# Head bits from four column tiles, TensorE's order rewritten, and a different start of a 16-head attention with two MLPs

## Chip, core and metric

The kernel runs on one core of one Trainium2 chip. The metric is the device time of one execution in microseconds (us).

## What is computed

Attention whose mask comes from hashing: queries and keys are projected on six directions, the signs of the projections are six bits, and a query sees only the keys with the same six bits. Two MLPs follow. In the reference (cut):

```python
# batch 2, heads 8, sequence 768, head_dim 64; x is (1536, 512)
q_bits = (np.einsum('bhsd,dk->bhsk', q, proj) > 0)          # 6 bits, k the same
mask = q_bucket[:, :, :, None] == k_bucket[:, :, None, :]
scores = np.where(mask, (1/8) * np.matmul(q, k.T), -1e9)
attn = softmax(scores)
x = np.matmul(attn, v)                                       # heads side by side
h = np.maximum(np.maximum(x @ w1, x @ w2), x @ w3) @ w_out   # 512 -> 768 -> 512
g = h2 >= 1 ? h2 : h2 <= -1 ? 0 : (h2 + 1)**2 / 4            # h2 = h @ w_in, 512 -> 2048
return g @ w_out2                                            # 2048 -> 512
```

## The kernel before

**Stages.** The attention runs first (to about 189 us), the MLPs after it. A head (16 in all) has six tiles of 128 queries by 768 keys. Its inputs come as one array `r` with k in rows 0 to 63 and q in rows 64 to 127. Each number is split into a rounded part `hi` and a rest `lo`, so that products in the fast format keep their precision; `q`, `hi` and `lo` of a head are put together on 128 rows by transfers on SP's queue (`prep_both`: `q<-hi`, `prep_move`: `q<-lo`, `lo<-hi`).

**Bits.** `bits_both` multiplies `r` with the projection: two products of 384 columns each (a head's two halves), with 64 result rows each, in two column tiles of TensorE. `bits_rows` compares them on VectorE, once per half (44 rows by 384), and writes 44 rows of `q`; 12 of them are the query's bits and already in place, the key's 12 go to `hi` by one transfer on SP's queue (`hi<-q`, 12 rows by 768). The bits then stand as 12 more rows of the tile's product, where unequal bits add a huge number.

**A tile.** `t_qk` (L414, L417) makes four products of 384 columns in one of two PSUM buffers `s_ps`; `t_max` (VectorE, L424) takes the row's minimum and copies the tile out; `t_exp` (ScalarE, L439); then either six transposes (`t_tr`, L447, "t" below), copies out (`t_out`), and products with v (`g_pv`, L508, in two parts of 4 and 8 products with two passes each); or, for heads 2, 4, ... 14, a transpose on VectorE (`t_turn`) and one block of 96 small products (`block4`, L475: 32 rows by 64 columns of the array, 192 result columns each).

**Order.** A planner (`Work`) places tasks by costs and due times, but TensorE's own order is written out by hand in three strings (`first_part`, `period`, `last_part`): `q7` is the tile at place 7 of the sequence, `t7` its transposes, `v5` and `w5` the two parts of the products with v after tile 5, `b5` a head's bits, `B` head 1's bits, `r` a small transpose. The tile at place 6 is the first of head 1, that at place 10 the first of head 2, that at place 15 the first of head 3.

**Start.** TensorE first makes 13 products on zeros in bf16 (`warm_up`), while GpSimd changes signs in the projection `pj_raw` and scales it to `pj_sc`; head 0's two bit products follow, one after the other since both use the same column tile, then head 0's moves on ScalarE and GpSimd, with four more `warm_up` products between the first tile's own.

Of the kernel before, what the change touches and what calls it, by code (L numbers as in the profile page):

```python
# [8 lines left out]
F32 = mybir.dt.float32  # L9
# [4 lines left out]
ALU = mybir.AluOpType  # L14
# [8 lines left out]
HALF = S // 2  # L23
MASKED = 1.0e9
# [89 lines left out]
def lsh_attention_moe_kernel(  # L114
# [29 lines left out]
    pj_raw = const.tile([128, 64], F32, name="pj_raw")  # L144
# [3 lines left out]
    sc_sb = const.tile([128, 1], F32, name="sc_sb")  # L148
    one_exp = const.tile([128, 1], F32, name="one_exp")
# [131 lines left out]
    def attention(mlp_steps):  # L281
        with ExitStack() as ax, ExitStack() as sx:
# [24 lines left out]


# [18 lines left out]
            def pj_sign():  # L327
                for c0 in (0, 32):
                    nc.gpsimd.tensor_scalar(
                        out=pj_raw[:, c0:c0 + 6], in0=pj_raw[:, c0:c0 + 6], scalar1=-1.0, scalar2=0.0, op0=ALU.mult, op1=ALU.add  # L330
                    )
                nc.gpsimd.tensor_scalar(
                    out=pj_sc, in0=pj_raw, scalar1=sc_sb, scalar2=0.0, op0=ALU.mult, op1=ALU.add
                )
# [54 lines left out]
            def bits_mm(h, half, bank, first):  # L389
                nc.tensor.matmul(  # L390
                    out=bank[first:first + 64, 0:HALF], lhsT=pj_raw if h else pj_sc,
                    rhs=head[h]["r"][:, half * HALF:(half + 1) * HALF], start=True, stop=True,
                )
# [8 lines left out]
            def bits_both(h):  # L402
                for half in range(2):
                    bits_mm(h, half, pj_ps, 64 * half)


            def t_qk(n, bank):
# [3 lines left out]
                for half in range(2):  # L411
# [3 lines left out]
                    if n == 0:  # L415
                        warm_up(4, half)
# [73 lines left out]
            ahead = s_ps[1][:, 0]  # L490
# [107 lines left out]
            warm_up(13, 0)  # L598
            load_head(1)
            load_v(0)  # L600
            banks0 = (pj_ps, u_ps)
            halves = [slice(0, HALF), slice(HALF, S)]
            pj_sign()
            prep_hi_scaled(0, halves[0])
            bits_mm(0, 0, banks0[0], 64)
            prep_lo_scaled(0, 0, nc.vector)
            prep_move(0, "qb", nc.gpsimd.tensor_copy, halves[0])
            prep_hi_scaled(0, halves[1])
            bits_mm(0, 1, banks0[1], 64)
            prep_move(0, "qa", nc.scalar.copy, halves[0])  # L610
            prep_move(0, "ql", nc.scalar.copy, halves[0])
            prep_lo_scaled(0, 1, nc.vector)
            prep_move(0, "kh", nc.gpsimd.tensor_copy, halves[0])
            bits_rows(0, 0, banks0[0], 64)
            prep_move(0, "ql", nc.scalar.copy, halves[1])
            prep_move(0, "qb", nc.gpsimd.tensor_copy, halves[1])
            prep_move(0, "qa", nc.scalar.copy, halves[1])
            prep_move(0, "kh", nc.gpsimd.tensor_copy, halves[1])
            prep_move(0, "kb", nc.scalar.copy, halves[0])
            bits_rows(0, 1, banks0[1], 64)  # L620
            prep_move(0, "kb", nc.scalar.copy, halves[1])

            work = Work()
            T_AT, P_AT = 2, 1
            START = {h: min(SLOT[NK * h + t] for t in range(NK)) for h in range(NH)}
# [4 lines left out]
            SHIFT = {t_exp: 42.5, t_out: 2.0, g_copy: 17.5, copy4: -82.0, pair_copy: -20.5, w_tick: 60.0, bits_rows: 4.5, t_max: -12.5, t_turn: 8.0, pair_recip: 20.0}  # L630
# [8 lines left out]
            scaled, moves, r_place, order = {}, {}, {}, {}  # L639
            raw_s["prep"].free.pop()  # L640
            raw_s["r"].free.pop()

            def head_tasks(h):
# [17 lines left out]
                scaled[h], moves[h], r_place[h] = hi, [q, ql, kh], rp  # L661
                if h == 1:
                    bp = place("b", 1)
                    mm = task("PE", 0.644, due + 1, bits_both, h, after=[hi], takes=[bp], leaves=[rp])
                    order["bits"] = [mm]
                    rows = [
                        task("DVE", 0.69, due + 1, bits_rows, h, half, pj_ps, 64 * half, after=[mm]) for half in range(2)
                    ]
                    rows[1]["leaves"] = [bp]
                    bits_task(h, rows, due + 1)  # L670

            def bits_task(h, rows, due):
# [426 lines left out]
```

## Time and profile before

| | us |
|---|---|
| median of 3 runs (lowest, highest) | 667.93 (667.04, 668.33) |
| the profiled execution's own time | 668.48 |
| its span, first to last instruction | 666.6 |
| TensorE busy in the span | 657.4 |
| VectorE, ScalarE, GpSimd busy | 486.2, 341.0, 274.4 |

The difference of 1.9 us between the execution's time and its span lies around the program. PE is TensorE, DVE VectorE, ACT ScalarE, POOL GpSimd, SP the engine that issues most transfers. TensorE's products are pipelined: a row's time includes the last product's way through the array, so what a step takes is read from its start to the next row's start. A float32 product is two passes and shows as two records.

### The profile page before, as it was taken

How to read it: one execution, taken by the hardware profiler on the slowest of the kernel's cores; microseconds unless marked ns; L12 is line 12 of the kernel's file. 1: busy time of each engine (PE TensorE's matmuls, PEld its weight loads, DVE VectorE, ACT ScalarE, POOL GpSimd, SP SyncE). 2: the span in 40 equal slices, each digit the busy share in tenths (PEclk: the TensorE clock that was granted, in tenths of full speed). 3: DMA queues.
4: the chain of work that ended last, by engine and by line, in shares of the span. 5: the costliest groups of instructions: out<-in, count | busy, mean ns of one | idle time of the engine just before them, and what ended most of it. 6: DMA issues, size and time to landing. Idle time of an engine off the chain costs nothing.

```text
span 666.6 us, 11523 instructions
## 1 busy us (share of the span) xinstructions
PE 657.4 (99%) x4419; PEld 527.4 (79%) x4419; DVE 486.2 (73%) x717; ACT 341.0 (51%) x633; POOL 274.4 (41%) x249
## 2 busy tenths in 40 slices
PE   8999999999999999999999999999999999999998
PEld 5667777777867888888888888888888888888886
DVE  5787989998863667875453466766888888888844
ACT  7787877887782233333222325665444444444430
POOL 5436556766322335344223113644444444444430
PEclk9999999999999999999999999999999999999999
DMA  6847787775243122322111122121111222211004
GB/s 194 221 122 185 199 217 197 186 243 140 83 135 81 64 95 72 119 70 65 47 49 56 55 73 86 42 71 57 63 64 64 63 65 63 64 63 64 32 0 190
DMA packets 27855, 66.99 MB, mean 100 GB/s; under 512 B 4164, under 2 KB 9124, under 8 KB 27800
## 3 DMA queue, kind: packets, MB, share of 16 engines
q1 hardware_dynamic: 27488, 66.21, 33.8%
q8 instruction: 35, 0.57, 0.4%
q14 instruction: 20, 0.16, 0.1%
q10 hardware_dynamic: 312, 0.04, 0.0%
HBM read 46.17 MB, written 3.19 MB: 74 GB/s over the span
## 4 chain that ended last, share of the span: by engine, by line
PE 96%; issue 1%; DVE 1%; DMA 1%; ACT 1%; SPq 0%; POOL 0%; POOLq 0%; DVEq 0%
PE b L270 49%; PE b L1017 20%; PE s_ps L414 6%; PE t_ps L447 5%; PE u_ps L508 5%; PE s_ps L417 5%; PE u_ps L475 3%; PE pj_ps L390 2%; PE t_ps L475 1%; DVE p L424 1%; DMA rb<-d 0%; PE pj_ps L475 0%; ACT p L439 0%; PE s_ps L270 0%; DMA d<-rt 0%
## 5 line engine op out<-in xcount | busy, mean ns | idle before, releaser
L270 PE MATMUL b<-x_hl,wx 128*128 128x512 f32 x684 | 159.6, 389 | 0.0
L270 PEld LDWEIGHTS b<-x_hl,wx 128*128 128x128 f32 x684 | 128.4, 188 | 26.6
L270 PE MATMUL b<-x_hl,w 128*128 128x512 f32 (+1 forms) x564 | 123.8, 376 | 0.0
L270 PEld LDWEIGHTS b<-x_hl,w 128*128 128x128 f32 x564 | 100.9, 188 | 19.8 <-issue 0.6
L917 POOL TENSOR_TENSOR g<-r,g 128x512 fp32r<-128x512 f32 x48 | 62.5, 1304 | 121.4 <-ACT g L916 121.4
L424 DVE TENSOR_SCALAR_CACHE_REDUCE p<-s_ps 128x768 f32<-128x768 f32 x96 | 89.7, 951 | 11.9 <-PE s_ps L417 8.7
L206 DVE SCALAR_TENSOR_TENSOR wg<-wg,wr 128x512 f32<-128x512 f32 (+1 forms) x58 | 67.3, 1160 | 37.6 <-ACT wg L204 36.9
L439 ACT ACTIVATE p<-p,nm 128x768 f32<-128x768 f32 x96 | 89.7, 936 | 5.6 <-DVE p L424 5.1
L414 PE MATMUL s_ps<-lo,q 128*128 128x384 f32 x192 | 72.0, 375 | 1.0 <-DVE p L424 0.9
L233 POOL TENSOR_TENSOR wx<-wg,wx 128x512 fp32r<-128x512 f32 (+1 forms) x32 | 45.6, 1426 | 65.3 <-ACT wx L227 48.4
L1017 PE MATMUL b<-wx,g 128*128 128x512 f32 x288 | 72.1, 389 | 0.0
L1017 PE MATMUL b<-w,g 128*128 128x512 f32 (+1 forms) x294 | 71.3, 385 | 0.0
L227 ACT CAST wx<-wg 128x512 fp32r<-128x512 f32 (+1 forms) x32 | 19.3, 604 | 92.6 <-DVE wg L219 92.6
L417 PE MATMUL s_ps<-hi,q 76*128 76x384 f32 x192 | 65.3, 340 | 0.0
L997 DVE SCALAR_TENSOR_TENSOR r<-r,b 128x512 f32<-128x512 f32 x48 | 33.0, 687 | 44.3 <-ACT r L996 44.3
L1017 PEld LDWEIGHTS b<-w,g 128*128 128x128 f32 x294 | 54.5, 188 | 11.1
L1017 PEld LDWEIGHTS b<-wx,g 128*128 128x128 f32 x288 | 54.1, 188 | 11.2
L1024 DVE TENSOR_TENSOR acc<-b,acc 128x512 f32<-128x512 f32 (+1 forms) x85 | 56.3, 675 | 7.7 <-PE b L1017 7.6
L233 POOL TENSOR_TENSOR w<-wg,w 128x512 fp32r<-128x512 f32 (+1 forms) x26 | 35.9, 1382 | 49.3 <-ACT w L227 39.1
L211 DVE TENSOR_SCALAR wg<-wg 128x512 int32<-128x512 int32 (+1 forms) x58 | 53.3, 920 | 2.7
L995 ACT ACTIVATE r<-b,half_sb 128x512 f32<-128x512 f32 x48 | 33.0, 687 | 41.3 <-PE b L270 41.3
L227 ACT CAST w<-wg 128x512 fp32r<-128x512 f32 (+1 forms) x26 | 15.8, 608 | 74.0 <-DVE wg L219 74.0
(90 smaller groups left out, 1060.2 us busy)
## 6 DMA issues: line engine op xcount, KB each, us to landing
wr<-in_w SPq DMA_DIRECT2D x48, 512.0 KB
r<-in_kq SPq DMA_DIRECT2D x15, 384.0 KB
q<-hi SPq DMA_DIRECT2D x15, 384.0 KB
v<-in_v SPq DMA_DIRECT2D x21, 256.0 KB
rb<-d SPq DMA_DIRECT2D x16, 192.0 KB
wr<-in_w SPq DMA_DIRECT2D x8, 384.0 KB
q<-lo SPq DMA_DIRECT2D x15, 192.0 KB
lo<-hi SPq DMA_DIRECT2D x15, 192.0 KB
```

The source lines that it names most:

```text
L206: nc.vector.scalar_tensor_tensor(out=f32(g), in0=f32(g), scalar=TINY_SQ, in1=f32(high), op0=ALU.is_ge, op1=ALU.mult)
L211: nc.vector.tensor_scalar(out=g2, in0=g, scalar1=3, scalar2=0x3FFFFFF8, op0=ALU.logical_shift_left, op1=ALU.bitwise_and)
L227: nc.scalar.copy(out=w[:, 0, 0:cols], in_=f32(g2))
L233: nc.gpsimd.tensor_tensor(out=w[:, 1, 0:cols], in0=f32(g2), in1=f32(w[:, 0, 0:cols]), op=ALU.subtract)
L270: nc.tensor.matmul(out=outp, lhsT=w_[a], rhs=x_[b_], start=(begins and i == 0 and jj == 0), stop=(ends and i == n - 1 and jj == 2),)
L414: nc.tensor.matmul(out=o, lhsT=hd["qa"][:, qs], rhs=hd["lo"][:, ks], start=True, stop=False)
L417: nc.tensor.matmul(out=o, lhsT=hd["qb"][0:76, qs], rhs=hd["hi"][0:76, ks], start=False, stop=True)
L424: nc.vector.tensor_scalar(out=p.rearrange("p (a k) -> p a k", a=2), in0=s_ps[bank.at][:, :, 0:HALF], scalar1=MASKED, scalar2=MASKED, op0=A ...
L439: nc.scalar.activation(out=p, in_=p, func=ACTF.Exp, scale=-1.0, bias=tl[n]["nm"], accum_out=sums_of(h // 2)[:, c:c + 1],)
L917: nc.gpsimd.tensor_tensor(out=dst[:, 1, cs], in0=src, in1=f32(dst[:, 0, cs]), op=ALU.subtract)
L1017: nc.tensor.matmul(out=pb[:, cs], lhsT=gs[f][:, a, tsl], rhs=wt[:, b_, cs], start=(n == 0), stop=(n == len(terms) - 1),)
L1024: nc.vector.tensor_tensor(out=acc[:, t, cs], in0=pb[:, cs], in1=acc[:, t, cs], op=ALU.add)
```

## The change

1. A head's bits come from four products of 192 columns with 32 result rows each, in four column tiles (`bits_four`), and two comparisons of 56 rows by 192 columns (`bits_two`). Three transfers of 12 rows by 2 x 192 take the rows to their places (`bits_move`) where one of 12 rows by 768 did. The products wait for the scaled `r` alone.
2. The three strings of TensorE's order, the planner's costs and its shifts of due times are new.
3. Head 0's projection `pj_sc` is one product on GpSimd (with a sign and scale table `pj_by` that is set beforehand); its two bit products use different column tiles; the moves behind it stand in another order, and one of them is on GpSimd instead of ScalarE.
4. The 13 bf16 products at the start become 29 rounds of four float32 products on zeros (32 rows, 64 columns, 64 result columns; `warm_small`), and one `warm_up` product instead of four stands between the first tile's products.

```diff
+            def warm_small(rounds):
+                zeros = f32(warm)
+                for _ in range(rounds):
+                    for q in range(4):
+                        rows = slice(32 * q, 32 * q + 32)
+                        nc.tensor.matmul(
+                            out=quarter(q)[UP, HALF + 64:512], lhsT=zeros[rows, 0:64], rhs=zeros[rows, 64:128],
+                            start=True, stop=True,
+                        )
...
-            def bits_both(h):
-                for half in range(2):
-                    bits_mm(h, half, pj_ps, 64 * half)
+            def bits_four(h):
+                for c in range(4):
+                    nc.tensor.matmul(
+                        out=pj_ps[32 * c:32 * c + 32, 0:QUART], lhsT=pj_raw[:, 64:96],
+                        rhs=head[h]["r"][:, c * QUART:(c + 1) * QUART], start=True, stop=True,
+                    )
+            def bits_two(h, half):
+                rows = slice(64 * half, 64 * half + 56)
+                nc.vector.tensor_scalar(
+                    out=head[h]["qb"][64:120, half * HALF:half * HALF + QUART], in0=pj_ps[rows, 0:QUART],
+                    scalar1=pc_sb[rows, 2:3], scalar2=pc_sb[rows, 3:4], op0=ALU.is_gt, op1=ALU.mult,
+                )
+            def bits_move(h, to, at, odd):
...
+                nc.sync.dma_start(out=side(hd[to], slice(64, 76), odd), in_=side(hd["qb"], slice(at, at + 12), 0))
...
-            warm_up(13, 0)
+            warm_small(29)
...
+            nc.gpsimd.tensor_tensor(out=pj_sc, in0=pj_raw[:, 0:64], in1=pj_by, op=ALU.mult)
+            for half, bank in enumerate((pj_ps, u_ps)):
+                bits_mm(0, half, bank, 64 * half)
+                prep_hi_scaled(0, halves[half])
...
-                "q0 q1 B q2 t0 q3 q4 t1 t2 q5 b5 t3 v2 w2 t4 q6 q11 b8 t5 q7 q8 t6 v5 w5 q9 t7 q10 q12 t8 "
+                "q0 q1 q2 B t0 q3 t1 q4 b5 t2 q5 t3 v2 t4 b8 q6 t5 q7 w2 q8 t6 q11 v5 q10 t7 q9 w5 q12 t8 "
...
```

The order on TensorE around the first tile of head 2 (operands `lo_251`, `q_252` in the first piece, `lo_353`, `q_354` in the second; the other tiles there are head 1's). Before:

```order
L447 MATMUL t_ps_119<-ident_84,p_329 128x128 x6
L508 MATMUL u_ps_85<-pt_293,vr_139 64x384 x6
L414 MATMUL s_ps0_116<-lo_187,q_188 128x384
L417 MATMUL s_ps0_116<-hi_186,q_188 128x384
L414 MATMUL s_ps0_116<-lo_187,q_188 128x384
L417 MATMUL s_ps0_116<-hi_186,q_188 128x384
L447 MATMUL t_ps_119<-ident_84,p_366 128x128 x6
L414 MATMUL s_ps1_117<-lo_251,q_252 128x384
L417 MATMUL s_ps1_117<-hi_250,q_252 128x384
```

Now:

```order
L440 MATMUL s_ps1_122<-hi_287,q_289 128x384
L531 MATMUL u_ps_86<-pt_394,vr_247 64x384 x2
L437 MATMUL s_ps0_121<-lo_353,q_354 128x384
L440 MATMUL s_ps0_121<-hi_352,q_354 128x384
L437 MATMUL s_ps0_121<-lo_353,q_354 128x384
L440 MATMUL s_ps0_121<-hi_352,q_354 128x384
L470 MATMUL t_ps_124<-ident_85,p_451 128x128 x6
L437 MATMUL s_ps1_122<-lo_288,q_289 128x384
L440 MATMUL s_ps1_122<-hi_287,q_289 128x384
L437 MATMUL s_ps1_122<-lo_288,q_289 128x384
L440 MATMUL s_ps1_122<-hi_287,q_289 128x384
L531 MATMUL u_ps_86<-pt_394,vr_247 64x384 x4
```

Four of the six products with v, one tile of head 1 and six transposes that stood ahead of head 2's first tile now stand behind it.

SP's queue over the same stretch, from the bits of head 1 to those of head 2 (each `r<-in_kq` loads a head, `q<-hi`, `q<-lo` and `lo<-hi` are a head's moves). Before:

```order
L379 DMA hi<-q 12x768
L385 DMA q<-hi 64x2x768
L379 DMA lo<-hi 64x768
L379 DMA q<-lo 64x768
L313 DMA r<-in_kq 128x768
L325 DMA v_180<-in_v 128x512
L385 DMA q<-hi 64x2x768
L379 DMA hi<-q 12x768
L379 DMA lo<-hi 64x768
L379 DMA q<-lo 64x768
```

Now, from behind head 1's own three bit transfers:

```order
L386 DMA lo<-hi 64x768
L392 DMA q<-hi 64x2x768
L386 DMA q<-lo 64x768
L325 DMA r<-in_kq 128x768
L337 DMA v_281<-in_v 128x512
L392 DMA q<-hi 64x2x768
L386 DMA lo<-hi 64x768
L386 DMA q<-lo 64x768
L428 DMA hi<-q 12x2x192
L428 DMA q<-q 12x2x192
L428 DMA hi<-q 12x2x192
```

Head 2's bits were the third transfer from the end of this piece; they are three now, and stand behind head 3's `q<-lo`.

## Rows read from the trace of the kernel before

**Rows 1.** The page: busy time by engine, and the queue of instruction refills.
```profile
PE 657.4 (99%) x4419; PEld 527.4 (79%) x4419; DVE 486.2 (73%) x717; ACT 341.0 (51%) x633; POOL 274.4 (41%) x249
...
q8 instruction: 35, 0.57, 0.4%
```

**Rows 2.** Windows: stretch, length, busy (x instructions) of PE, PEld, DVE, ACT, POOL; clock; DMA.
```profile
29.20:188.90 159.70, 156.83 (x1947) 117.77 (x1945) 140.05 (x252) 125.16 (x248) 86.39 (x95) 1.00 0.65 173
...
300.00:500.00 200.00, 200.00 (x884) 165.68 (x883) 122.32 (x161) 84.36 (x149) 69.77 (x54) 1.00 0.19 60
```

**Rows 3.** TensorE's waits, 0 to 190 us: total us, times, longest us.
```profile
PE pj_ps L475 <- issue: 1.2, 1, 1.2
...
PE t_ps L447 <- ACT pt L457: 1.0, 1, 1.0
PE s_ps L414 <- DVE p L424: 0.9, 1, 0.9
...
PE u_ps L475 <- issue: 0.5, 1, 0.5
```

**Rows 4.** Timeline of the start: start us, us, engine, line, out<-in.
```profile
1.05 2.96 PE L306 MATMUL t_ps<-warm 128*128 128x256 bf16 x13 [1.05 <-DVE half_sb L1048]
...
3.61 0.37 POOL L329 TENSOR_SCALAR pj_raw<-pj_raw 128x6 f32<-128x6 f32 x2 [3.17 <-DMA pj_raw<-in_pj]
4.07 0.74 POOL L332 TENSOR_SCALAR pj_sc<-pj_raw,sc_sb 128x64 f32<-128x64 f32 x1
...
4.87 0.86 PE L390 MATMUL pj_ps<-r,pj_sc 128*64 128x384 f32 x2 [0.85 <-POOL pj_sc L332]
...
6.41 0.69 DVE L397 TENSOR_SCALAR q<-u_ps,pc_sb 44x384 fp32r<-44x384 f32 x1
...
6.59 1.12 ACT L381 CAST hi<-q 12x384 fp32r<-12x384 f32 x2
...
8.02 0.44 PE L417 MATMUL s_ps<-hi,q 76*128 76x384 f32 x1
...
8.50 0.96 DVE L424 TENSOR_SCALAR_CACHE_REDUCE p<-s_ps 128x768 f32<-128x768 f32 x1 [1.40 <-PE s_ps L417]
```

**Rows 5.** Timeline of TensorE around a head's bits.
```profile
16.19 0.87 PE L390 MATMUL pj_ps<-r,pj_raw 128*64 128x384 f32 x4
16.98 0.87 PE L447 MATMUL t_ps<-ident,p 128*128 128x128 f32 x6
17.79 2.16 PE L508 MATMUL u_ps<-pt,vr 128*64 128x384 f32 x12
19.87 0.87 PE L447 MATMUL t_ps<-ident,p 128*128 128x128 f32 x6
```

**Rows 6.** Timeline of TensorE in a block of small products.
```profile
80.95 0.32 PE L475 MATMUL u_ps<-dt,v 32*64 32x192 f32 x1
...
81.27 0.32 PE L475 MATMUL u_ps<-dt,v 32*64 32x192 f32 x1
```

**Rows 7.** Groups on VectorE, 8 to 189 us: count, busy us, mean ns of one, idle before.
```profile
L397 DVE TENSOR_SCALAR q<-pj_ps,pc_sb 44x384 fp32r<-44x384 f32 x30 | 20.4, 678 | 2.0 <-ACT p L439 0.9 <-ACT pt L457 0.2
```

**Rows 8.** Timelines of SP's queue, TensorE and GpSimd around head 2's first tile.
```profile
21.59 0.59 SPq L379 DMA_DIRECT2D q<-lo  x1
...
23.01 0.45 SPq L313 DMA_DIRECT2D r<-in_kq  x1
...
27.84 0.45 PE L414 MATMUL s_ps<-lo,q 128*128 128x384 f32 x1
...
29.23 0.42 PE L414 MATMUL s_ps<-lo,q 128*128 128x384 f32 x1
...
30.65 0.83 POOL L338 TENSOR_SCALAR r<-r 64x768 f32<-64x768 f32 x1 [2.76 <-DMA r<-in_kq]
```

**Rows 9.** Timelines of SP's queue and TensorE around head 8's first tile.
```profile
93.99 0.80 SPq L379 DMA_DIRECT2D hi<-q  x1
...
98.27 0.42 PE L414 MATMUL s_ps<-lo,q 128*128 128x384 f32 x1
```

More of the change, by code (lines that the diff above doesn't have):

```diff
@@ L23 @@
 HALF = S // 2
+QUART = S // 4
 MASKED = 1.0e9
@@ L327, in pj_sign @@
             def pj_sign():
[L328 to L334, printed above, removed]
+                rows = pj_raw[:, 64:88].rearrange("p (a b) -> p a b", a=2)[:, :, 0:6]
+                nc.gpsimd.tensor_scalar(out=rows, in0=rows, scalar1=-1.0, scalar2=0.0, op0=ALU.mult, op1=ALU.add)
             def prep_scale(h, eng):
@@ L390, in bits_mm @@
                 nc.tensor.matmul(
-                    out=bank[first:first + 64, 0:HALF], lhsT=pj_raw if h else pj_sc,
+                    out=bank[first:first + 64, 0:HALF], lhsT=pj_sc,
                     rhs=head[h]["r"][:, half * HALF:(half + 1) * HALF], start=True, stop=True,
@@ L660, in head_tasks, with bits_tasks @@
                 kh = task("SP", 0.5, due + 2, prep_move, h, "kh", after=[ql], lag=3.5)
-                scaled[h], moves[h], r_place[h] = hi, [q, ql, kh], rp
+                scaled[h], moves[h], r_place[h] = sc, [q, ql, kh], rp
+                placed[h] = hi
                 if h == 1:
                     bp = place("b", 1)
[L664 to L672, printed above, removed]
-                q, ql, kh = moves[h]
-                ready[h] = [task("SP", 0.8, due, prep_move, h, "kb", after=rows + [q], lag=2.5), q, ql, kh]
+                    order["bits"] = [bits_tasks(h, due + 1, due + 1, due + 1, bp)]
+            def bits_tasks(h, due, due_rows, due_move, bp):
+                mm = task("PE", 0.48, due, bits_four, h, after=[scaled[h]], takes=[bp], leaves=[r_place[h]])
+                rows = [task("DVE", 0.42, due_rows, bits_two, h, half, after=[mm, placed[h]]) for half in range(2)]
+                rows[1]["leaves"] = [bp]
+                rows[1]["after"].append(rows[0])
+                q, ql, kh = moves[h]
+                ready[h] = [
+                    task("SP", 0.5, due_move + 0.1 * j, bits_move, h, *x, after=rows + [q, placed[h]], lag=2.5)
+                    for j, x in enumerate((("hi", 76, 0), ("qb", 96, 1), ("hi", 108, 1)))
+                ] + [q, ql, kh]
+                return mm
             def v_tasks(h):
@@ L723, in tile_tasks @@
                 for half in range(2):
-                    tr = task("PE", 0.288, m - 4, t_tr, n, half, after=[ex, tr], takes=[] if half else [tb], leaves=[pp], lag=0.1)
+                    tr = task("PE", 0.327, m - 4, t_tr, n, half, after=[ex, tr], takes=[] if half else [tb], leaves=[pp], lag=0.1)
                     order[f"tr{n}"] = order.get(f"tr{n}", []) + [tr]
@@ L742, in group_tasks @@
                 if bits:
-                    bm = task("PE", 0.644, m + 0.4, bits_both, bits, after=[scaled[bits]], takes=[bp], leaves=[r_place[bits]])
-                    order[f"bits{g}"] = [bm]
-                    rows = [task("DVE", 0.69, m - 3, bits_rows, bits, half, pj_ps, 64 * half, after=[bm]) for half in range(2)]
-                    rows[1]["leaves"] = [bp]
-                    rows[1]["after"].append(rows[0])
-                    bits_task(bits, rows, START[bits] - 6)
+                    order[f"bits{g}"] = [bits_tasks(bits, m + 0.4, m - 3, START[bits] - 6, bp)]
                 last = None
@@ L1068 @@
     v4 = np.tile(v.reshape(B * H, NB, 32, D).transpose(0, 2, 1, 3), (1, 4, 1, 1))
[L1069 to L1070 removed]
+    pj = np.zeros((128, 96), proj.dtype)
+    for rows, c0 in ((slice(0, 64), 32), (slice(64, 128), 0), (slice(0, 64), 76), (slice(64, 128), 64)):
         pj[rows, c0:c0 + 6] = proj
@@ L1076 @@
     for rows, first, top in ((0, edge, 1.0), (6, past, 1.0), (32, past, BIG), (38, edge, BIG)):
-        pc[rows:rows + 6] = pc[rows + 64:rows + 70] = [first, top, -0.5 if first > 0 else 0.5, 0.5 * top]
+        pc[rows:rows + 6, 0:2] = pc[rows + 64:rows + 70, 0:2] = [first, top]
+        for at in range(rows % 32 + (12 if top > 1 else 0), 128, 32):
+            pc[at:at + 6, 2:4] = [first, top]
     mw = {n: np.asarray(a) for n, a in inputs.items() if n.startswith("moe")}
```

77 lines of the change are left out of this document (37 added, 40 removed), and 3 rows, old and new, of the table first_part.

## The prediction

> **What bounds the kernel now.** I read the page first: TensorE is busy 657.4 of 666.6 us, with VectorE 486.2 behind it, and its instructions are refilled in 35 fetches [rows 1]. The windows say where the rest is: in the MLPs TensorE is busy 200.0 of 200.0 us, in the attention from 29.2 to 188.9 us 156.8 of 159.7 [rows 2]. The change touches the attention alone, so the end moves by as much as TensorE's work and waits in the first 190 us do; the MLPs follow at the same pace whenever they start. TensorE's own waits there are few [rows 3]: 1.0 us for ScalarE's copies, 0.9 us for VectorE's row minimum, and gaps of 1.2 and 0.5 us ("issue", nothing released them) inside the blocks of small products. So there are hardly any waits to win, only work, and work is worth its price only where TensorE does not then wait for something else. The start is the exception: there a chain over five engines ends in the first row minimum at 8.50 us [rows 4], which I call T.
>
> **Bits: TensorE.** Two products of 384 columns in two column tiles, two passes each, take 0.80 us (16.19 to 16.98), and three times as many products 2.09 us (17.79 to 19.87) [rows 5]. So four more pair-passes cost 1.29 us: one pass of 384 columns, both tiles side by side, is 0.32 us, and 0.16 us of a step is fixed. Four tiles of 192 columns would need two passes of 0.16 us if all four run side by side: 0.48 us, 0.32 less. Full height with four column tiles is not in this trace. The bounds: two at a time, 0.80 us (no gain); one after the other, 1.44 us (0.64 more). The nearest row is the block of small products, where two batches of eight tiles (four row groups by two column groups, 192 columns) take 0.32 us [rows 6], a full 0.16 us pass for each batch. I take 0.48. For 15 heads that is at most 4.8 us. The bits of heads 1 to 3 stand ahead of head 2's first tile, in a stretch whose end is set by something else (below); 12 x 0.32 = 3.84 us remain.
>
> **Bits: VectorE.** Thirty comparisons of 0.68 us [rows 7] become thirty at half the columns: between 0.34 and 0.68, I take 0.5, about 5 us of VectorE in all. TensorE waits for VectorE for 0.9 us only, so I book nothing; it covers the tighter pace.
>
> **Head 2's first tile.** It starts at 29.23 us, T + 20.7. The last of head 2's transfers goes out just ahead of head 3's `q<-lo`, which is issued at 21.59. Transfers are slow there: the `r` issued at 23.01 is taken up at 30.65 by GpSimd, which had stood idle 2.76 us for it, so it took some 7 us [rows 8]. At that pace head 2's last transfer lands at about 27.8 us, 1.4 us before the tile needs them. Two things change. In TensorE's order the larger part of a group of products with v (four pair-passes and the fixed part, 1.44 us by [rows 5]) and a tile with six transposes (27.84 to 29.23, 1.39 us [rows 8]) move behind this tile: it is reached 2.8 us earlier, at T + 17.9. I book no gain on top for the three heads' bits and the 1.0 us wait ahead of it, since that wait shows ScalarE's copies setting the pace there. In SP's queue head 2's bits, now three transfers, stand behind head 3's `q<-lo`: they land no earlier than its 21.59 + 7 = 28.6, T + 20.1, and with two more small transfers behind it I take T + 20.5. TensorE then waits 2.6 us. Behind it the 0.9 us wait for VectorE vanishes, since VectorE catches up meanwhile. Net +1.7 us. Bounds: if transfers land in 3 us, no wait and 0.9 gained; if each of the extra four costs 0.8 of SP's time in series, +3.5.
>
> **Start.** The bits of head 0 start at 4.87 us, held by `pj_sc` (three instructions on GpSimd from 3.61, 0.37 + 0.74 us); from there to T are 3.63 us [rows 4]. Now one instruction makes `pj_sc`: between 0.2 and 0.74 us, ready at 3.9 to 4.4. But the small products on zeros stand ahead. Thirteen bf16 products of 256 columns take 2.96 us [rows 4], about 0.21 each, one column per 0.83 ns: the 1.2 GHz level. A pass of 192 float32 columns at 2.4 GHz is 0.16 us [rows 6], so one of 64 columns is 0.054, and 0.108 at 1.2 GHz; 29 rounds are 58 passes, 3.1 us at the one, 6.3 us at the other. The rise of the clock falls between 4 and 5 us here, if the small products raise it as the large did; with 2.85 us at the slow level (26 passes) and 32 passes at the fast one they end at 1.05 + 2.85 + 1.7 = 5.6 us. The bits start 0.75 us later. Behind them VectorE's two comparisons in a row set the pace as before (the second ends 7.10), and so do ScalarE's moves, to 7.71 [rows 4]; the last product of the first tile started 0.3 later, at 8.02, behind four warm products, of which one is left. That gives back 0.25: T + 0.5. Bounds: all at the fast level, bits at 4.3, -0.8; all at the slow one, bits at 7.4, +2.3.
>
> **Order and queues.** The products with v are now in 23 steps instead of 20; each step's fixed part is 0.16 us: +0.5. Thirty more transfers on SP cost it 0.5 to 0.8 us each, 15 to 24 us of 190; I book none of it, as long as bits come early enough (rival two). The gaps in the blocks stay (+-1.2).
>
> **Sum.** -3.84 + 1.7 + 0.5 + 0.5 = -1.1 us on the profiled execution's 668.48, which stands 0.55 above the median of the runs shown: 666.8.
>
> **A rule of the skill on the start.** The refills are one for about 252 weight loads and products (8,838 over 35 fetches) [rows 1]; 29 rounds are 464 of them in the first few us, nearly two refills. The Trainium skill ("Runtime: NRT & Kernel Launch", Instruction fetch mechanics) says that TensorE holds 2,048 instructions and is refilled in blocks of 256, crossing a block being mostly hidden; by that the start would not wait for a refill, and the sum stays at 666.8. The block size agrees with the 252; the "issue" gaps of up to 1.2 us in the densest stretches [rows 3] speak for much less in store, and with a like gap the sum would be 668.0.
>
> **Rivals.** (1) *The start waits for instructions*, or for the clock: 464 instructions are spent before a refill has come, or the small products don't raise the clock. For it: the gaps in the blocks, where 384 instructions run in some 4 us. Against: nothing is known of what is in store at the start. Price 1.2 to 1.8 us: 668.0 to 668.6, no change. (2) *SP's queue makes every head late* (slower). Head 8's bits are issued at 93.99 and its first tile starts at 98.27 [rows 9], 4.28 us later. Two further issues at 0.8 us leave 2.7; shorter products and comparisons give back 0.3 + 0.4. If a landing takes longer than these 3.4 us, each later head's first tile waits. At 0.3 us a head (12 heads, 3.6 us) the gain of the bits is gone: 670.4; at 0.6 it is 674. Against: TensorE's new order may place the bits earlier relative to the tile. (3) *Head 2 doesn't wait*: the load of head 2 and its moves also start earlier, transfers are less crowded. Then 2.6 us less: 664.2. (4) *The four tiles don't run side by side*, the change doesn't do what it says: 670.6 if in pairs, 680 if one after the other.
>
> **Chances.** Forecast (665.3 to 668.3) 0.40; rival 1 0.17; rival 2 0.12; rival 3, partly with a faster start, 0.25; rival 4 0.06. A measurement here tells about 0.2% (1.3 us) from no change: faster means below 666.6, slower above 669.3. Of the forecast's 0.40, 0.18 is faster; with rival 3, and a little where both start and head 2 go half as well, 0.45 is faster; rivals 2 and 4 and some of 1 make 0.22 slower; 0.33 remain. The range takes in rival 3 (with a start at its fast bound 663.5) and the pairs of rival 4 (670.6), not a wait at every head.
>
> **What would show it.** Right: from the start of a head's bits to the next step 0.48 us; comparisons near 0.5; T near 9.0; TensorE waiting 2 to 3 us at the first tile of head 2 for a transfer. Wrong: bits at 0.80; an "issue" gap at the end of the small products; T at 8 or beyond 10; waits for transfers at one head after another.

## The result, and the profile after

| kernel | median us (lowest to highest), runs | ratio to before, 95% interval |
|---|---|---|
| before | 667.99 (667.04 to 668.65), 6 | |
| changed | 675.56 (674.17 to 679.02), 6 | 1.0121 (1.0094 to 1.0148) |

The change makes the kernel 1.2% slower; the forecast of 666.8 us and its range, up to 670.6, missed it. The profiled execution of the changed kernel took 679.02 us, the longest of the six, 3.5 above their median; against the profiled one of before (668.48) it loses 10.5 us, and the bookkeeping below is for that pair.

The page of the changed kernel answers to [rows 1]: TensorE's busy time hardly moved, its span grew by 10.6 us.

```profile
span 677.2 us, 12139 instructions
PE 659.0 (97%) x4692; PEld 530.0 (78%) x4692; DVE 480.1 (71%) x718; ACT 338.9 (50%) x631; POOL 273.1 (40%) x253
...
q8 instruction: 37, 0.61, 0.4%
...
PE 88%; DMA 4%; SPq 2%; DVE 2%; issue 2%; ACT 0%; POOL 0%; POOLq 0%; DVEq 0%; ACTq 0%
```

The last line is the chain of work that ended last, by engine: TensorE carries 88% of it; transfers, their issue on SP, and gaps that nothing shown released ("issue") make up 8%. The page of before has 96% and 2%:

```profile
PE 96%; issue 1%; DVE 1%; DMA 1%; ACT 1%; SPq 0%; POOL 0%; POOLq 0%; DVEq 0%
```

The products and comparisons did what they were to do. In the timeline TensorE's next step starts 0.46 us behind a head's bits (0.80 before, [rows 5]):

```profile
13.53 0.53 PE L411 MATMUL pj_ps<-r,pj_raw 128*32 128x192 f32 x8
13.99 0.55 PE L470 MATMUL t_ps<-ident,p 128*128 128x128 f32 x3
```

and the comparisons take 478 ns instead of 678 [rows 7] (groups on VectorE, 8 to 200 us):

```profile
L418 DVE TENSOR_SCALAR q<-pj_ps,pc_sb 56x192 fp32r<-56x192 f32 x30 | 14.3, 478 | 1.0 <-issue 0.2
```

The loss is in what stands around them. TensorE's waits, from the first row minimum on (12 to 206 us; total us, times, longest), answer to [rows 3]:

```profile
PE pj_ps L498 <- issue: 3.7, 2, 2.2
PE s_ps L440 <- DMA hi<-q: 2.3, 3, 1.1
PE t_ps L498 <- issue: 1.3, 1, 1.3
PE s_ps L437 <- DMA q<-q: 1.1, 1, 1.1
PE s_ps L437 <- DVE p L447: 1.0, 2, 0.7
PE t_ps L470 <- ACT pt L480: 1.0, 3, 0.5
PE u_ps L531 <- DMA vr<-in_v: 0.6, 1, 0.6
```

Transfers, for which the rows of before show no wait, now hold TensorE for 4.0 us (2.3 + 1.1 + 0.6), and the gaps inside the blocks of small products grew from 1.7 us to 5.0. At the start (timeline, [rows 4] before) the small products stop for 2.2 us shortly before their end, and the first row minimum comes at 11.61 us instead of 8.50:

```profile
5.74 0.22 PE L315 MATMUL t_ps<-warm 32*64 32x64 f32 x2
7.91 0.21 PE L315 MATMUL pj_ps<-warm 32*64 32x64 f32 x1 [1.95 <-issue]
...
8.19 0.54 PE L397 MATMUL pj_ps<-r,pj_sc 128*64 128x384 f32 x1
...
10.43 0.44 PE L440 MATMUL s_ps<-hi,q 76*128 76x384 f32 x1 [0.88 <-ACT hi L388]
...
11.61 0.96 DVE L447 TENSOR_SCALAR_CACHE_REDUCE p<-s_ps 128x768 f32<-128x768 f32 x1 [1.13 <-PE s_ps L440]
```

The queue that refills instructions moves its first block just then (the row is of the window from 4.9 to 6.6 us), and none from there to 9.0 us:

```profile
q8 instruction: 1, 0.02, 5.9%
```

At head 2's first tile ([rows 8] before) TensorE waits for the last two bit transfers, one after the other:

```profile
28.96 0.87 PE L531 MATMUL u_ps<-pt,vr 128*64 128x384 f32 x4
30.89 0.41 PE L437 MATMUL s_ps<-lo,q 128*128 128x384 f32 x1 [1.07 <-DMA q<-q]
32.19 0.41 PE L440 MATMUL s_ps<-hi,q 76*128 76x384 f32 x1 [0.88 <-DMA hi<-q]
```

And the clock, at full speed through the whole attention before [rows 2], falls to its lower level (1.2 GHz) twice. The windows show it (length, busy of PE, PEld, DVE, ACT, POOL; granted clock; DMA share, GB/s): in front of the first fall TensorE had been busy 1.32 of the 3 us from 103 to 106, waiting for transfers; in front of the second it stood still 1.5 us in a block of small products (last row, from the timeline). The longest stop, 2.2 us in the first block, was followed by no fall (granted clock 1.00 from 4.2 to 106.6 us). The profile is one execution of six; the mean granted clock of the six is 0.994 to 0.997, so each of them lost something.

```profile
103.00:106.00 3.00, 1.32 (x8) 0.70 (x9) 2.01 (x4) 1.87 (x5) 1.66 (x2) 1.00 0.65 200
...
106.60:110.00 3.40, 3.40 (x12) 1.53 (x9) 0.70 (x1) 1.33 (x3) 1.66 (x2) 0.50 0.94 239
110.00:168.00 58.00, 54.31 (x847) 42.23 (x847) 49.58 (x91) 42.45 (x86) 36.72 (x41) 1.00 0.73 193
168.10:171.40 3.30, 3.30 (x20) 2.49 (x18) 1.67 (x4) 1.81 (x4) 2.44 (x3) 0.50 0.61 157
```

```profile
166.61 0.32 PE L498 MATMUL pj_ps<-dt,v 32*64 32x192 f32 x1 [1.49 <-issue]
```

The books for the 10.5 us: start +3.1; gaps in blocks +3.3 (5.0 - 1.7); transfers +4.0; 6.8 us at half speed +3.4; bits -5.0 (15 heads by 0.333 us). That is +8.8; the three more steps with v are some 0.5, and 1.2 are not assigned. The MLPs take the same time in both (458.3 and 458.2 us from their first product to the end of the span), so all of it is lost ahead of them, as the prediction said.

### The profile page after: what moved, and what is told of

Read it like the earlier page. It is cut to its first block, busy times and chain, and to the rows that moved or that the text cites. A ratio compares the mean times of both kernels' runs of the same rounds, so it can differ in the third digit from the quotient of the medians.

```text
span 677.2 us, 12139 instructions
## 1 busy us (share of the span) xinstructions
PE 659.0 (97%) x4692; PEld 530.0 (78%) x4692; DVE 480.1 (71%) x718; ACT 338.9 (50%) x631; POOL 273.1 (40%) x253
## 4 chain that ended last, share of the span: by engine, by line
PE 88%; DMA 4%; SPq 2%; DVE 2%; issue 2%; ACT 0%; POOL 0%; POOLq 0%; DVEq 0%; ACTq 0%
PE b L272 48%; PE b L1037 19%; PE s_ps L437 4%; PE u_ps L531 4%; PE t_ps L470 4%; PE s_ps L440 4%; PE u_ps L498 3%; DMA hi<-q 1%; PE t_ps L498 1%; SPq L428 1%; DVE p L447 1%; DMA lo<-hi 1%; PE pj_ps L411 1%; PE u_ps L315 1%; DMA q<-lo 1%
## 5 line engine op out<-in xcount | busy, mean ns | idle before, releaser
L221 DVE SCALAR_TENSOR_TENSOR wg<-wr,wg 128x512 int32<-128x512 int32 (+1 forms) x58 | 52.2, 901 | 0.9
```

The costliest lines, as they stand in the source:

```text
L221: nc.vector.scalar_tensor_tensor(out=g2, in0=low, scalar=29, in1=g2, op0=ALU.logical_shift_right, op1=ALU.bitwise_or)
```

## The experiments

Each kernel was timed in five rounds beside the kernel before (its medians there 667.6 to 668.1). The ratio is not that of the medians, so the two differ by up to 0.2%. "First minimum" is the start of the first row minimum in the profile, which is one execution.

| run | median us (lowest to highest) | ratio, 95% interval | first minimum |
|---|---|---|---|
| 1: 13 rounds | 670.61 (670.19 to 673.75) | 1.0052 (1.0029 to 1.0074) | 8.09 |
| 2: 11 rounds | 671.42 (669.45 to 677.01) | 1.0058 (1.0035 to 1.0080) | 8.27 |
| 3: new bits in the kernel before | 677.84 (677.37 to 678.29) | 1.0149 (1.0129 to 1.0169) | 8.53 |
| 4: changed, old start | 675.31 (670.87 to 678.68) | 1.0115 (1.0079 to 1.0151) | 10.02 |
| 5: 13 rounds, head 2 later | 675.70 (673.70 to 678.92) | 1.0112 (1.0087 to 1.0138) | 8.75 |
| 6: 13 rounds, kh first | 673.07 (672.33 to 675.05) | 1.0075 (1.0056 to 1.0094) | 9.55 |
| 7: 11 rounds, both | 675.04 (673.69 to 678.87) | 1.0108 (1.0081 to 1.0134) | 9.60 |
| 8: 13 rounds, old bits | 673.45 (672.11 to 674.75) | 1.0069 (1.0051 to 1.0087) | 8.61 |
| 9: new start in the kernel before | 669.74 (668.21 to 670.07) | 1.0010 (0.9997 to 1.0023) | 9.00 |
| 10: changed, 13 bf16 products | 671.00 (669.20 to 673.62) | 1.0043 (1.0026 to 1.0060) | 8.19 |
| 11: run 3, two queues | 678.68 (676.84 to 681.76) | 1.0163 (1.0135 to 1.0192) | 8.42 |
| 12: run 1, planner's old numbers | 674.16 (671.19 to 678.26) | 1.0088 (1.0057 to 1.0118) | 8.35 |
| 13: before, split blocks | 672.81 (672.56 to 674.72) | 1.0078 (1.0065 to 1.0092) | 8.68 |
| 14: run 1, split blocks | 676.84 (676.38 to 678.98) | 1.0138 (1.0121 to 1.0156) | 8.52 |
| 15: before, two more transfers | 679.10 (675.83 to 683.06) | 1.0164 (1.0134 to 1.0194) | 10.25 |
| 16: run 10, kh first, split blocks | 677.74 (675.31 to 678.99) | 1.0141 (1.0122 to 1.0161) | 9.65 |
| 17: run 3, transfers in one piece | 676.04 (674.92 to 677.66) | 1.0130 (1.0113 to 1.0146) | 8.62 |
| 18: run 1, transfers in one piece | 671.17 (669.35 to 675.51) | 1.0070 (1.0047 to 1.0093) | 9.21 |

### The start and the refills (runs 1, 2, 4, 9, 10)

Run 1 changes one number, run 2 takes 11:

```diff
-            warm_small(29)
+            warm_small(13)
```

> The changed kernel with 13 rounds of small products at the start instead of 29; 16 rounds are 256 weight loads and products, so the refills fall on the same places of the later blocks. Theory A (what TensorE loses at the start comes out at the end): no gap at the end of the small products, head 0's bits start at 4.2 to 4.5 us instead of 8.19, first row minimum at 7.6 to 8.3 us instead of 11.61, the three gaps in the blocks of small products stay (together 5 to 7 us), time 671.5 to 672.5. Theory B (SP's transfers set the pace): the first row minimum comes as early, but head 2's first tile waits longer for its transfers, and the time stays above 674.5.

> The same with 11 rounds: 32 weight loads and products fewer than with 13, so that in the seven blocks of small products only one block still has two refill boundaries more than a few instructions inside it. Theory A: start as with 13 rounds; the gaps in the blocks shrink from 6 us to at most 2.5, the second fall of the granted clock (behind the gap at 164.8 us) is gone, which is worth 1.7: time 665 to 667.5. Theory A2 (the gaps are not refills but waits for something in the blocks): gaps stay where they are, time equal to 13 rounds within 0.7. Theory B: the gaps go, waits for transfers grow in their place, time above 670.

Run 1 bears out theory A on the start, and the time falls further than it said, by 5.0 us (the intervals of the ratios are apart). The gap is gone; what holds the first product now is a move on GpSimd (`kh` in the code, head 0's `lo<-hi`):

```profile
4.74 0.68 PE L397 MATMUL pj_ps<-r,pj_sc 128*64 128x384 f32 x1
...
6.81 0.44 PE L437 MATMUL s_ps<-lo,q 128*128 128x384 f32 x1 [1.39 <-POOL lo L388]
```

The gaps in the blocks stand where refills put them. In the changed kernel they follow record 183 of the 192 of the first block (a product is two), 178 of the third and 174 of the fifth; with 16 rounds (256 weight loads and products) less they follow the same three records, and with 32 fewer again (run 2) that of the fifth block follows record 190 and those of the first and third, which would come at 199 and 194, are gone. The rows behind the first block's gap, changed kernel and run 1, and behind the fifth's in run 2 (timelines):

```profile
67.15 0.37 PE L498 MATMUL pj_ps<-dt,v 32*64 32x192 f32 x1 [2.24 <-issue]
```

```profile
63.99 0.37 PE L498 MATMUL pj_ps<-dt,v 32*64 32x192 f32 x1 [1.37 <-issue]
```

```profile
159.86 0.32 PE L498 MATMUL pj_ps<-dt,v 32*64 32x192 f32 x1 [1.35 <-issue]
```

So the gaps go with the count of instructions in steps of 256, and each of these seven ends 2.4 to 3.1 us after the refill queue began to move a block: they are refills, and A2 falls. But run 2 is not faster than run 1, and waits for transfers did not grow as theory B said (0.8 us after 2.2). Its gaps in the blocks are smaller, 1.5 us by the waits against 4.6 (and 0.9 right behind a block), but its clock, up at 4.9 us, fell again behind the wait for the same move, and stayed low for 6.7 us (windows):

```profile
4.90:8.30 3.40, 1.77 (x12) 1.10 (x9) 2.04 (x4) 2.90 (x6) 2.62 (x6) 1.00 0.81 267
8.40:15.10 6.70, 6.70 (x30) 5.01 (x29) 4.29 (x9) 4.68 (x10) 5.48 (x6) 0.50 0.72 194
```

Run 4 puts the start of the kernel before into the changed one, run 10 only its 13 bf16 products, and run 9 puts the new start, without its small products, into the kernel before:

```diff
-            warm_small(29)
+            warm_up(13, 0)
...
-            nc.gpsimd.tensor_tensor(out=pj_sc, in0=pj_raw[:, 0:64], in1=pj_by, op=ALU.mult)
-            for half, bank in enumerate((pj_ps, u_ps)):
-                bits_mm(0, half, bank, 64 * half)
...
+            pj_first()
+            prep_hi_scaled(0, halves[0])
+            bits_mm(0, 0, banks0[0], 64)
```

> The changed kernel with the start of the kernel before (13 bf16 products, three GpSimd instructions for pj_sc, moves in the old order). Theory A: first row minimum at 8.5 us (3.1 less); refill boundaries in the first 45 instructions of five blocks and at 129 and 385 of one, gaps of 0 to 2 us instead of 6, no fall of the clock behind the sixth block; waits for transfers at heads 2 and 8 stay: 665 to 668.5. If the time is within 0.5 of the run with 11 rounds, the new start as such (one product, two column tiles) is worth nothing. Theory B: above 670.

> The kernel before with part 3 of the change alone: pj_sc by one product, head 0's bit products in two column tiles, its moves in the new order; the 13 bf16 products, bits, order and planner as before. Theory A (the shorter chain comes out at the end): head 0's bits start at 4.1 to 4.5 us instead of 4.87 and stand side by side, first row minimum at 7.5 to 8.0 instead of 8.50, time 667.0 to 667.6 against 668.0. Theory B (the moves on GpSimd or the later rise of the clock set the first tile): first row minimum at 8.4 or later, 668 to 669.5.

> The changed kernel with 13 bf16 products in place of the 29 rounds, all else as changed. Refill boundaries stand 16 to 57 weight loads and products inside four blocks. Theory A (the start and the refills in the blocks are the loss): no gap at the start, first row minimum at 7.8 to 8.4 us, gaps in the blocks 1 to 4 us in all instead of 6.4, at most one fall of the clock: 667 to 669.5. Theory B (the new order's own waits for transfers and copies are the rest): 670 to 673, as with 13 or 11 rounds.

Run 4 is inconclusive: its times spread over 8 us, and they part by the clock (in the other runs the two go together only loosely). The three executions with a mean granted clock of 1.000 took 670.9 to 673.9 us, the three with 0.995 to 0.997 took 676.8 to 678.7. In its profile the clock rose only at 8.8 us. (The record of the clock begins with its first rise; windows ahead of that read 1.00, so the rise is seen in the rows: four warm products take 0.98 us at 8.02 and 0.61 at 9.19.) Head 0's first bit product, in the kernel before 0.69 us to the next (4.87 in [rows 4] to 5.56, first row), takes 1.34 in run 4 (the others), and the first minimum stands at 10.02:

```profile
5.56 0.81 PE L390 MATMUL u_ps<-r,pj_sc 128*64 128x384 f32 x2
```

```profile
4.77 1.54 PE L406 MATMUL pj_ps<-r,pj_sc 128*64 128x384 f32 x2 [0.76 <-POOL pj_sc L348]
6.11 1.49 PE L406 MATMUL u_ps<-r,pj_sc 128*64 128x384 f32 x2
...
8.02 0.98 PE L308 MATMUL t_ps<-warm 128*128 128x256 bf16 x4
...
9.19 0.61 PE L308 MATMUL t_ps<-warm 128*128 128x256 bf16 x4
```

Run 9: the bits start at 4.21 us and stand side by side as theory A said, but the first product waits for the move of `kh` on GpSimd until 7.08 (theory B), and by the ratio (0.1%, with 1 inside the interval) the time cannot be told from before, though the medians stand 1.6 us apart. So in the kernel before, part 3 of the change by itself gains nothing that can be measured. Run 10 is theory B: first minimum and gaps (2.1 us) came as A said, but TensorE still waits 1.9 us for `hi` transfers, 1.2 for row minima and 1.7 for copies, the clock falls twice, and the time is 671.0. It differs from run 4 by part 3 and by one `warm_up` product instead of four inside the first tile, and is 4.3 us faster with intervals that are apart; whether the new start is worth that in the new order, or run 4's late rise and falls of the clock make the difference, is open.

### The bits and their transfers (runs 3, 8, 11, 15, 17, 18)

Run 3 takes the kernel before with the products, comparisons and transfers of the new bits. Run 15 takes the kernel before with its own bits and adds two transfers of the new form, ahead of the one that TensorE needs; they write rows that nothing reads. In the cut the first two lines are run 3's, the last three run 15's:

```diff
-                    mm = task("PE", 0.644, due + 1, bits_both, h, after=[hi], takes=[bp], leaves=[rp])
+                mm = task("PE", 0.48, due, bits_four, h, after=[scaled[h]], takes=[bp], leaves=[r_place[h]])
...
+                more = [task("SP", 0.5, due, spare_move, h, i, after=rows + [q], lag=2.5) for i in range(2)]
-                ready[h] = [task("SP", 0.8, due, prep_move, h, "kb", after=rows + [q], lag=2.5), q, ql, kh]
+                ready[h] = [task("SP", 0.8, due, prep_move, h, "kb", after=rows + [q] + more, lag=2.5), q, ql, kh]
```

> The kernel before with the new bits alone (four products, two comparisons, three transfers); start, order and planner as before. Theory A: 15 heads by 0.333 us, 5.0 us less; the refill boundaries move to the first 32 instructions of the blocks, gaps 0 to 1.5 instead of 2.8; no fall of the clock: 661 to 664. Theory B (three transfers make heads late): first tiles of several heads wait for the bits' transfers, 0.3 to 0.6 us each, time 666 to 670.

> The kernel before, bits and all, with two more transfers a head of 12 rows by 2 x 192 on SP's queue ahead of the one that brings the key's bits; they write rows that nothing reads. Theory A (the transfers on SP's queue are what makes heads late, as with the new bits in the old order, 677.8): TensorE waits 3 to 7 us in all for the key's bits at first tiles, time 671 to 677. Theory B (something else in the new bits does): waits for hi below 1.5 us, 668 to 670.

Theory B of run 3 and theory A of run 15 hold, by more than their numbers: 10.0 us slower with the new bits, 11.4 with the old bits and two more transfers. TensorE's waits, run 3 and run 15:

```profile
PE s_ps L449 <- DMA hi<-q: 5.4, 5, 2.2
PE t_ps L507 <- issue: 2.4, 2, 1.5
```

```profile
PE s_ps L424 <- DMA hi<-q: 6.6, 6, 2.8
PE t_ps L454 <- ACT pt L464: 1.1, 2, 1.0
```

The transfers in the traces fit this: from the issue of a head's first bit transfer to the landing of its last it takes 3.2 us before (median of 15 heads, one transfer), 5.1 in run 3 and 5.2 in the changed kernel (three transfers, of which the third goes out 2.4 and 3.0 us behind the first, since SP issues others between). In the old order a head's bits stand so close to its first tile that two more microseconds make the tile late. Run 15 does more than add two issues: since `more` stands in `after` with a lag of 2.5, the planner also places the needed transfer at least that long behind them, and in the trace it goes out 4.6 us behind the first (median; run 3's third 2.4). In its profile the clock rose only at 9.2 us and the first minimum stands at 10.25. So its 11.4 us are not the price of two issues alone.

Run 8 puts the old bits into run 1 (of its edit only the products are shown; comparisons and transfer change with them):

```diff
-                for c in range(4):
+                for c in range(2):
                     nc.tensor.matmul(
-                        out=pj_ps[32 * c:32 * c + 32, 0:QUART], lhsT=pj_raw[:, 64:96],
+                        out=pj_ps[64 * c:64 * c + 64, 0:HALF], lhsT=pj_raw[:, 0:64],
```

> The changed kernel with 13 rounds and the bits of the kernel before (two products of 384 columns, two comparisons of 44 rows by 384, one transfer), in the new order. Theory A (the four tiles' 0.333 us a head come out at the end): 15 by 0.333 us of TensorE more, 674 to 676 against 670.6. Theory B (two transfers fewer a head give back as much): waits at heads 2 and 8 shrink, 670 to 672.5.

Between the two: 2.8 us slower than run 1 by the medians, 1.1 by the ratios (0.17%), whose intervals overlap. TensorE's 5.0 us for the bits are there, but with one transfer a head it waits 0.5 us for transfers instead of 2.2 (waits of run 1, then of run 8). About half of the bits' gain, or less, comes out even in the new order, and since the intervals overlap it may be none.

```profile
PE s_ps L440 <- DMA hi<-q: 1.4, 2, 0.8
PE s_ps L437 <- DMA q<-q: 0.8, 1, 0.8
```

```profile
PE u_ps L527 <- DMA vr<-in_v: 0.5, 1, 0.5
```

Run 11 sends the second and third transfer of run 3 through ScalarE:

```diff
-                    for j, x in enumerate((("hi", 76, 0), ("qb", 96, 1), ("hi", 108, 1)))
+                    for j, (q_, x) in enumerate((("SP", ("hi", 76, 0)), ("ACT", ("qb", 96, 1, nc.scalar)), ("ACT", ("hi", 108, 1, nc.scalar))))
```

> The kernel before with the new bits alone, as in the run that took 677.8 us, but the second and third of a head's bit transfers are issued by ScalarE instead of SP. Theory A (what is late is the third issue, behind the other two and behind what SP puts between them): the third lands about 1 us earlier or more, TensorE's waits for hi and q at first tiles fall from 5.4 us to 2.5 or less: 673 to 675.5. Theory B (a landing takes as long on either queue, because the data path is busy): waits stay within 1.5 us, 676 to 679.

Theory A was right on the wait and wrong on the time, which lies in theory B's range: TensorE waits for no bit transfer any more, but for ScalarE, in whose order the issues (and their waits for the comparisons) now stand between exponentials and copies:

```profile
PE t_ps L479 <- ACT p L471: 4.1, 9, 1.5
PE u_ps L540 <- ACT pt L489: 2.1, 4, 0.6
PE t_ps L479 <- DVE pt L489: 1.3, 1, 1.3
```

Runs 17 and 18 give the quarters to the tiles in the order 0, 2, 1, 3, so that each transfer is one piece:

```diff
-                        rhs=head[h]["r"][:, c * QUART:(c + 1) * QUART], start=True, stop=True,
+                        rhs=head[h]["r"][:, (2 * (c % 2) + c // 2) * QUART:(2 * (c % 2) + c // 2 + 1) * QUART], start=True, stop=True,
...
-                nc.sync.dma_start(out=side(hd[to], slice(64, 76), odd), in_=side(hd["qb"], slice(at, at + 12), 0))
+                nc.sync.dma_start(out=f32(hd[to][64:76, cs]), in_=f32(hd["qb"][at:at + 12, 0:HALF]))
```

> The kernel before with the new bits alone (677.8 us), but the four tiles take the quarters of a head in the order 0, 2, 1, 3, so that each of the three transfers moves 12 rows of 384 numbers in one piece instead of two pieces of 192. Theory A (SP's time goes into the pieces): an issue takes 0.5 to 0.6 us instead of 0.85, the waits for hi fall from 5.4 to at most 3 us, 672 to 675.5. Theory B (the number of transfers counts): issue and waits stay, 676.5 to 679.

> The changed kernel with 13 rounds (670.6 us) and the same order of the quarters, transfers of 12 rows by 384 in one piece. Theory A: waits for hi and q at first tiles fall from 2.2 us to at most 1, 668 to 669.8. Theory B: 670 to 672.

An issue takes 0.78 us instead of 0.84 on the mean, so SP's time goes by the number of transfers and hardly by their form. The waits fell (in run 17 from 5.4 to 1.3 us, in run 18 to none for bits), the time hardly: run 17's gaps in the blocks grew to 4.6 us, and the intervals overlap with those of runs 3 and 1. Neither theory of run 17 holds; run 18's time is theory B's. Runs 11 and 17 take most of run 3's waits for bit transfers away and stay 8 to 11 us behind the kernel before, so taking these waits away does not give the 10 us back. TensorE's waits in run 17:

```profile
PE t_ps L505 <- issue: 4.6, 3, 3.0
...
PE s_ps L447 <- DMA hi<-q: 1.0, 3, 0.6
```

### The order (runs 5, 6, 7, 12, 13, 14, 16)

Run 5 moves head 2's first tile back, run 6 changes head 0's moves, run 7 does both with 11 rounds:

```diff
-                "q0 q1 q2 B t0 q3 t1 q4 b5 t2 q5 t3 v2 t4 b8 q6 t5 q7 w2 q8 t6 q11 v5 q10 t7 q9 w5 q12 t8 "
+                "q0 q1 q2 B t0 q3 t1 q4 b5 t2 q5 t3 v2 t4 b8 q6 t5 q7 w2 q8 t6 q11 v5 w5 q9 t7 q10 q12 t8 "
...
+            prep_move(0, "kh", nc.gpsimd.tensor_copy, halves[0])
+            prep_move(0, "qb", nc.gpsimd.tensor_copy, halves[0])
```

> The changed kernel with 13 rounds at the start, and in TensorE's order head 2's first tile (q10) back behind w5, q9 and t7, where the kernel before has it. With 13 rounds alone TensorE waits 1.3 and 1.2 us at this tile for head 2's last transfers, the clock falls to half behind it for 3.4 us, and the time is 670.6. Theory A (the wait and the fall are the cost of the early tile): both waits and this fall of the clock are gone, 2.1 and 1.6 us, of which up to 1.1 come back as a wait for VectorE as in the kernel before: 667 to 669. Theory B (the wait only moves to the next tile): 670 or more.

> The changed kernel with 13 rounds, and head 0's moves on GpSimd in another order: the first half of kh, for which the first tile's first product waits 1.4 us with 13 rounds, comes first. Theory A: that product starts at 5.5 to 6.2 us instead of 6.8, the first row minimum at 7.5 to 7.8 instead of 8.1, time 669.8 to 670.3. Theory B (ScalarE's copies of the bits set the row minimum): it stays at 8.0 or later, time as with 13 rounds within 0.4.

> The changed kernel with 11 rounds, head 2's first tile at its old place, and kh first. With 11 rounds alone the clock is at half from 8.4 to 15.2 us, behind a gap of 2.2 us for kh, and the time is 671.4. [...] Theory B (the new order is paced by ScalarE and VectorE anyway): 668 or more, with their waits grown.

No repair gained anything. Run 5 is theory B, and worse: the waits at head 2 are gone, and a tile behind it waits for GpSimd as long (first row); `hi` at a later head costs 1.4, and the time rises by 5.1 us over run 1's with no overlap of the intervals:

```profile
PE s_ps L437 <- POOL lo L374: 2.0, 1, 2.0
PE s_ps L440 <- DMA hi<-q: 1.4, 1, 1.4
```

In run 6 the first product no longer waits for `kh`, but in that profile the clock rose only at 13.9 us, and the first minimum stands at 9.55; neither theory gave its time. Run 7 has the same wait for GpSimd (2.0 us) and the same late clock (13.6 us); its time lies in theory B's range, but the waits for ScalarE and VectorE did not grow (1.0 and 1.1 us, in run 2 2.0 and 1.0).

Run 12 keeps the new strings and takes the planner's costs and shifts from the kernel before, as in this line:

```diff
-                mx = task("DVE", 0.9, m, t_max, n, sp, after=[qk], takes=[pp], leaves=[sp], lag=0.13)
+                mx = task("DVE", 1.04, m, t_max, n, sp, after=[qk], takes=[pp], leaves=[sp])
```

> The changed kernel with 13 rounds, the new strings of TensorE's order and the new bits, but the planner's costs, extra costs and shifts of the kernel before. Theory A (the strings, which put the bits earlier, take the waits for the bits' transfers away): 669.5 to 672.5, as with 13 rounds (670.6). Theory B (the planner's numbers do, by the order on SP and VectorE): first tiles of several heads wait again, 674 or more.

674.2, at the edge of theory B, with intervals that overlap run 1's: transfers cost 4.0 us here (bits 2.9, others 1.1), a comparison 1.8, and the clock is at half for 10.2 us. With the new bits the old order takes 677.8 us, the new one without the 29 rounds 670.6 to 671.0. But these also differ in the start. Run 4, which differs from run 3 in the order and the planner's numbers only, has 1.1 us of waits for bit transfers instead of 5.4 (and 1.4 for another transfer), while its time (675.3) is not told from run 3's by the intervals. So the new order takes waits away; what it gains in time, and how much of that is the strings, is not settled.

Runs 13, 14 and 16 put a tile's products between the two halves of each block but the last:

```diff
-                "q22 q24 v19 w19 t21 q25 q26 v20 w20 q27 t23 q30 q28 t25 b25 q29 q35 t27 v25 w25 q31 r25 "
+                "q22 q24 v19 w19 t21 q25 q26 v20 q27 w20 t23 q30 q28 t25 b25 q29 q35 t27 v25 w25 q31 r25 "
```

> The kernel before with one edit: in each block of small products but the last, one tile's four products stand between its two halves, so that the refill of instructions has 0.7 us more. Theory A (the gaps in the blocks are refills that come too late): the gaps of 0.8, 0.5 and 1.6 us shrink to 0 to 0.8 in all; seven more changes of step cost up to 1.1: 666.0 to 667.5 against 668.1. Theory B (VectorE or ScalarE sets the pace there, and the gaps cover it): 668 to 670, with waits for VectorE at the tile between.

> The changed kernel with 13 rounds and the same split of the blocks. With 13 rounds alone the gaps in the blocks take 5.6 us and the clock falls once behind the largest; time 670.6. Theory A: gaps 0.5 to 2.5 us in all, no fall of the clock behind a block: 666 to 668.5. Theory B (their place is taken by other waits): 669.5 or more.

> The changed kernel with the 13 bf16 products, kh first on GpSimd, and the split blocks. With the 13 bf16 products alone: first row minimum 8.19 us, gaps in the blocks 3.3, 671.0. Theory A: first row minimum 7.6 to 7.9, gaps in the blocks at most 1.5, one fall of the clock less: 666 to 668.5, level with the kernel before or better. Theory B (waits for transfers and copies move in): 669.5 or more.

The refills' gaps are all but gone in the three (0.6 us in run 16), and the kernels are slower by 5 to 7 us (theory B in runs 14 and 16, more than either theory in run 13). The tile that moved into the block had hidden ScalarE's copy of the block's result, for which the transposes behind it now wait, six times in run 13:

```profile
PE t_ps L447 <- ACT u L488: 3.9, 6, 0.7
```

In run 14 the same wait (4.1 us) and 3.9 us for `hi` transfers; in run 16 4.0 and 2.2, and half speed for 10.2 us. No version beat the kernel before.

## Why the prediction was wrong

**Bits on TensorE and VectorE: right.** 0.463 us a head (0.48 said), comparisons 0.48 (0.5). Rival 4 is out.

**Start: wrong, and the largest single piece.** "T + 0.5", bounds -0.8 and +2.3; measured T + 3.1. The pace of the small products was right (the clock rose at 4.2 us, and all but a few had gone out by 5.74); the step that failed is that they would go out without a stop. Rival 1 came in, 2.2 us instead of its 1.2 to 1.8. The gap stands 223 passes into the 232 of the 29 rounds, that is after some 446 weight loads and products. The Trainium skill ("Runtime: NRT & Kernel Launch", Instruction fetch mechanics) puts 2,048 instructions in TensorE's store and calls the crossing of a block mostly hidden. The trace disagrees: 2.2 us after some 446. Run 1 shows what the 29 rounds cost: 5.0 us of the 7.6.

**"The gaps in the blocks stay (+-1.2)": wrong.** From 1.7 to 5.0 us. The reason was at hand: some 430 more weight loads and products at the start, and 8 more a head, shift the places of the refills, and the sum left them where they were.

**The clock: not in the sum beyond the start.** Two falls, 3.4 us; in the kernel before the clock stood at full speed through the whole attention once it had risen.

**"I book none of it" for SP's thirty transfers: wrong.** Put into the old order, the new bits with their transfers cost 10.0 us (run 3) where 5.0 of TensorE's work were saved; which part of that the transfers have is not shown, since run 15 also delays the needed one and runs 11 and 17 took the waits away without the time. In the changed kernel 4.0 us of waits for transfers are left, half of them at head 2, where they were booked, the rest near 104 and 154 us: rival 2, given 0.12, came in at a part of its price. Of the bits' 5.0 us at most about half is left where the two forms are compared in one order (run 8).

**Head 2: right in place and about in size.** Waits of 2.0 us for 2.6 said, and the wait for VectorE behind it vanished.

**Two slips that change nothing.** The text puts the clock's rise between 4 and 5 us; its sum uses 3.9, which is what the trace has. Rival 4's 680 counts 15 heads, its 670.6 counts 12; with 12 the first is 678.3.

**Sum.** TensorE's work fell as booked. The step that failed is the one under the whole sum, that TensorE's waits elsewhere would stay as they were: +0.5 us for the start measured +3.1, the gaps in the blocks +3.3 instead of 0, the clock +3.4 instead of 0, transfers behind head 2 +2.0 instead of 0 (all in the profiled pair, of which the changed one is the longest of six). Only the start's price is shown in time (run 1). The prices of transfers, refills and clock are read from the traces alone; runs 2, 13 and 14 removed gaps and gained nothing. Open is how the 2.8 us by which run 1's median still stands above that of before beside it divide among gaps, clock and transfers, and why repairs of the new order at one place (runs 5 and 6) cost more than the wait that they remove.

## What to carry to other kernels

Here one engine was busy 99% of the time in an order tuned by hand, and the price of the change was not the work that it took off this engine but what its small transfers, its instruction count and its gaps did to the rest. In such a kernel count issues on the queue and the time from first issue to last landing against the slack at each consumer. Warm-up work made of many small products uses up instructions that have to be fetched before the first real work; count it by instructions too, not by time alone. Where a wait was removed here by moving one step (runs 5, 11 and 13), another wait came up in its place, so look first at what stands ready behind it.

## What was not expected of the hardware

- TensorE waits 1.1 to 2.8 us inside three of the seven blocks of 384 weight loads and products (start to start, changed kernel and run 1), behind exactly the same record when 256 are taken away ahead of it.
- The granted clock of the same warm-up rose at 3.9 us in the kernel before and at 8.8 in run 4, which has the same start and a first row minimum 1.5 us later; with 13 rounds it rose at 5.1 in run 1 and at 13.9 in run 6. Run 4's six executions spread over 8 us, those of the kernel before over 1.6 to 4.0 in the comparisons.
